# Exp behind the state chain's copies, mixer rows loaded later, the last batch's angles moved forward: one change to a fused recurrence and mixer kernel

## The chip, the cores and the metric

The kernel runs on one core of a Trainium2 chip. The core has a matrix engine (PE, with its weight loads shown as PEld), a vector engine (DVE), an activation engine (ACT), a general engine (POOL), an engine that issues transfers (SP), and 16 DMA engines. Each engine works through its own instructions in order and waits for others by semaphores. The metric is the device time of one execution in microseconds (us), as the median of several runs.

## The reference

A recurrence over 768 steps runs for 4 batches of 8 heads with a 40 x 40 state per head; its output feeds a mixer. Cut to what matters:

```python
for t in range(S):
    y[:, :, t] = einsum('bhd,bhde->bhe', rt, state)
    Sa = einsum('bhde,bhe->bhd', state, at)
    state_decay = state * wt[:, :, None, :] - einsum('bhd,bhe->bhde', Sa, bt)
    state = state_decay + einsum('bhd,bhe->bhde', vt, kt)
x = y as [batch, token, 320]
theta = x @ w_theta
zr, zi = x * cos(theta), x * sin(theta)
u = x + einsum('ts,bsd->btd', w_tok_r, zr) + einsum('ts,bsd->btd', w_tok_i, zi)
out = u + maximum(u @ w_ch, 0)
```

The two token matrices are 768 x 768, the two channel matrices 320 x 320.

## The kernel before

The 768 steps of a batch are cut into 6 chunks of 128, so there are 24 tiles, numbered 0 to 23 through the batches, and a loop of 24 iterations (lines 516 to 564). A tile's recurrence is written as matrix products inside the chunk plus a state `gt` handed from tile to tile. The loop is a software pipeline: iteration i loads the raw inputs of tile i+4, takes logarithm and decay sums of tiles i+3 and i+2, forms the scores of tile i+1, does the state step of tile i, and finishes the output of tile i-1 and the mixer angles of tile i-2.

**Preparation of a tile.** `load` issues six transfers of 160 KB from SP into the `raw` pool (three buffers). `prep_ln` takes the Ln of w on ACT (`lw`). `prep_csi` sums it on PE (L148) and takes the Exp on ACT (`invW`, L151); POOL multiplies k and b by it (`kb`, L155). `prep_cse` does the same for a second sum (`Wi`, `ah`). `prep_rv` casts r and v on POOL (`rv`, L143). `tr_kb`, `tr_a`, `tr_rv` transpose on PE (all show as L182) and copy out (`kbT`, `aT`, `rvT`); scores are formed on PE (L214) and masked on DVE (L222).

**The state chain of a tile.** `rec_x0` builds a product on PE, whose negative ACT copies as `nx` (L273). `rec_nu` takes it back to PE (L278, L281), and ACT copies `nu` (L285). `rec_gt` makes the next state. `nx` of tile i marks the beginning of iteration i in what follows.

**The mixer.** `moe_theta` multiplies a tile with w_theta, and ACT copies the angles (`th`, L424). Three tiles' cosines and sines are taken together (`moe_sines`, L443) in iterations 4, 7, 10, 13, 16, 19 and 22; they need another ACT table than Ln and Exp, so a table load stands before them, and `ln_exp_again` (L447) loads the Ln and Exp table right behind them. An iteration later POOL multiplies them with x (`moe_z`, L432: `zr`, `zi`). A row block of the mixer output sums twelve products of `wtok` and z (`y_part`, L453); it is added to x (`u`), transposed (L362), copied (`uT`), multiplied with w_ch (L410) and written out (`oo`, two buffers). Batch b's rows are made while later tiles run, one row block in an iteration from iteration 9 on; the last batch's six rows are made behind the loop.

The token matrices arrive as six row blocks each. A row block of both, here called a pair, is loaded by two transfers that POOL issues (`wtok_load`), and three buffers hold each matrix's blocks. Two iterations later PE transposes them (`wtok_trans`, L399) and DVE copies the result.

**What sets the order.** The program is written in the order of the loop, but a scheduler orders each engine's instructions by priorities and estimated times, and may move them past each other. Instructions wrapped in `keep_in_program_order` keep their order among themselves. PSUM has four small buffers (`sm`) and two large ones (`sc`), which are handed out in turn. ACT, POOL and PE never overtake inside one engine: an instruction that waits holds everything behind it.

## Time and profile before

| what | value |
|---|---|
| median of 3 runs | 260.32 us (259.92 to 261.09) |
| the profiled execution's own time | 262.26 us |
| its span, from first to last instruction | 260.5 us |
| mean granted PE clock | 0.949 |
| PE busy | 215.0 us, 83% |
| DVE busy | 185.4 us, 71% |
| ACT busy | 160.4 us, 62% |
| POOL busy | 120.9 us, 46% |
| DMA moved | 30.81 MB, nearly all in packets under 512 B |

A row of a timeline gives the start in us, the time that the instruction was busy, the engine (a small q behind it means the engine's sequencer, as for issued transfers), the line, the operation, the tiles out<-in with their shapes, and in square brackets how long the engine had been idle and what ended that. Matmuls are pipelined: their busy times overlap, so the distance between starts tells the pace. The digit lines of the page cut the span into 40 slices of 6.5 us.

### The profile page before, as it was taken

How to read it: one execution, taken by the hardware profiler on the slowest of the kernel's cores; microseconds unless marked ns; L12 is line 12 of the kernel's file. 1: busy time of each engine (PE TensorE's matmuls, PEld its weight loads, DVE VectorE, ACT ScalarE, POOL GpSimd, SP SyncE). 2: the span in 40 equal slices, each digit the busy share in tenths (PEclk: the TensorE clock that was granted, in tenths of full speed). 3: DMA queues.
4: the chain of work that ended last, by engine and by line, in shares of the span. 5: the costliest groups of instructions: out<-in, count | busy, mean ns of one | idle time of the engine just before them, and what ended most of it. 6: DMA issues, size and time to landing. Idle time of an engine off the chain costs nothing.

```text
span 260.5 us, 8110 instructions
## 1 busy us (share of the span) xinstructions
PE 215.0 (83%) x3368; PEld 167.8 (64%) x3368; DVE 185.4 (71%) x287; ACT 160.4 (62%) x303; POOL 120.9 (46%) x186
## 2 busy tenths in 40 slices
...
DMA  7999999999999898767697579645500001011012
GB/s 128 189 176 149 210 158 195 159 159 169 181 190 168 138 172 154 133 117 136 129 172 138 91 137 169 113 95 110 103 29 4 28 25 35 20 64 40 0 50 101
DMA packets 155685, 30.81 MB, mean 118 GB/s; under 512 B 150401, under 2 KB 155649, under 8 KB 155649
## 3 DMA queue, kind: packets, MB, share of 16 engines
...
q0 software_dynamic: 2432, 2.77, 6.4%
q8 instruction: 26, 0.43, 0.7%
q14 instruction: 11, 0.08, 0.1%
...
## 4 chain that ended last, share of the span: by engine, by line
PE 46%; ACT 15%; issue 12%; DMA 10%; POOL 9%; DVE 4%; SPq 3%; POOLq 0%; DVEq 0%; ACTq 0%
PE sm L453 10%; DMA raw_rv<-in_r_dram 9%; PE sm L182 7%; PE sc L214 6%; PE sm L410 5%; ACT cs L443 4%; SPq L128 3%; ACT L443 2%; ACT L447 2%; PE sc L453 2%; PE sm L362 2%; PE sm L349 2%; PE sm L278 2%; DVE lamu L222 1%; POOL kb_93 L155 1%
## 5 line engine op out<-in xcount | busy, mean ns | idle before, releaser
L103 ACT COPY rvT<-sm 128x1024 bf16<-128x1024 bf16 x18 | 18.2, 1013 | 26.0 <-PE sm L182 26.0
L453 PE MATMUL sm<-zr,wtok_r 128*128 128x320 bf16 x120 | 33.8, 304 | 0.0
L453 PE MATMUL sm<-zi,wtok_i 128*128 128x320 bf16 x120 | 33.7, 303 | 0.0
L222 DVE TENSOR_TENSOR psi<-sc,mask_p 128x1024 bf16<-128x1024 f32 x24 | 29.3, 1221 | 5.4 <-PE sc L214 5.1
L222 DVE TENSOR_TENSOR phi<-sc,mask_n 128x1024 bf16<-128x1024 f32 x24 | 29.1, 1214 | 0.0
L222 DVE TENSOR_TENSOR lamu<-sc,mask_p 128x1024 bf16<-128x1024 f32 x24 | 29.1, 1214 | 0.0
L222 DVE TENSOR_TENSOR lamv<-sc,mask_p 128x1024 bf16<-128x1024 f32 x24 | 29.1, 1214 | 0.0
L193 DVE COPY kbT<-sm 128x1024 bf16<-128x1024 bf16 x24 | 16.5, 687 | 14.7 <-PE sm L182 14.7
L331 ACT COPY nuT<-sm 128x512 bf16<-128x512 bf16 x24 | 14.0, 585 | 10.9 <-PE sm L182 10.8
L453 PEld LDWEIGHTS <-wtok_r 128*128 128x128 bf16 x144 | 14.4, 100 | 9.6 <-issue 3.9
L453 PEld LDWEIGHTS <-wtok_i 128*128 128x128 bf16 x144 | 14.3, 100 | 7.5 <-issue 1.9
L214 PE MATMUL sc<-aT,kbT 64*128 64x128 bf16 x384 | 18.8, 229 | 0.0
L273 ACT ACTIVATE nx<-sm 128x320 bf16<-128x320 f32 x24 | 10.4, 432 | 11.5 <-PE sm L269 11.5
L103 ACT COPY uT<-sm 128x384 bf16<-128x384 bf16 x18 | 8.5, 483 | 14.1 <-PE sm L362 14.1
L143 POOL CAST rv_96<-raw_rv 128x320 bf16<-128x320 f32 x12 | 5.4, 453 | 24.5 <-DMA raw_rv<-in_r_dram 21.8
L155 POOL TENSOR_TENSOR kb_93<-raw_kb,invW 128x320 bf16<-128x320 f32 x12 | 10.1, 866 | 13.2 <-ACT invW L151 13.2
L424 ACT COPY th<-sm 128x320 f32<-128x320 f32 x24 | 10.6, 441 | 8.6 <-PE sm L410 8.6
L200 ACT COPY aT<-sm 128x512 bf16<-128x512 bf16 x24 | 14.1, 587 | 2.0 <-PE sm L182 2.0
L155 POOL TENSOR_TENSOR kb_91<-raw_kb,invW 128x320 bf16<-128x320 f32 x10 | 8.4, 861 | 14.4 <-ACT invW L151 14.4
L410 PE MATMUL sm<-wch,uT 128*128 128x320 bf16 x72 | 14.3, 313 | 0.2 <-ACT uT L103 0.2
L174 ACT ACTIVATE Wi<-sm 128x328 f32<-128x328 f32 x24 | 10.7, 448 | 5.9 <-PE sm L168 3.1
L214 PEld LDWEIGHTS <-kbT 64*128 64x128 bf16 x384 | 11.9, 99 | 3.7 <-issue 2.9
...
## 6 DMA issues: line engine op xcount, KB each, us to landing
...
wtok_row_r<-in_moe_w_tok_r_dram POOLq DMA_DIRECT2D x6, 192.0 KB, 5.1
```

Of the source, the lines that this page charges most:

```text
L103: nc.scalar.copy(out=out, in_=in_)
L155: (nc.vector if i < 2 else nc.gpsimd).tensor_tensor(out=q.kbh[:, j, :, 0:D], in0=q.kb[:, j], in1=q.invW[:, 0], op=ALU.mult)
L174: nc.scalar.activation(out=q.Wi, in_=cse[:, 0:DM + 8], func=AF.Exp)
L182: nc.tensor.transpose(out=dst[:, g * 128:(g + 1) * 128], in_=src[:, 2 * g:2 * g + 2, :].rearrange("p a b -> p (a b)"), identity=ident)
L193: nc.vector.tensor_copy(out=q.kbT.rearrange("p a b -> p (a b)"), in_=pt)
L200: nc.scalar.copy(out=q.aT, in_=pt[:, 0:512])
L214: nc.tensor.matmul(P[:, p, g, :], lhsT=lhs[rows(p), g * 128:(g + 1) * 128], rhs=rhs[rows(p), g * 128:(g + 1) * 128], start=True, stop=True)
L222: nc.vector.tensor_tensor(out=s.rearrange("p a b c -> p (a b) c"), in0=P.rearrange("p a b c -> p (a b) c"), in1=mask.to_broadcast([128, 2 ...
L331: nc.scalar.copy(out=q.nuT, in_=pt[:, 0:512])
L410: nc.tensor.matmul(dst, lhsT=lhs[:, kt, :], rhs=rhs[:, kt, :], start=kt == 0, stop=kt == 2)
L443: tc.keep_in_program_order(nc.scalar.activation(out=cs[:, c, 0:n], in_=ths[bi][:, j0:j0 + n], func=AF.Sin, bias=(pi2_col[:, :], 0.0)[c]))
L453: nc.tensor.matmul(yp, lhsT=wtok[nm][:, sb, j * 128:(j + 1) * 128], rhs=z[:, sb], start=start and n == 0, stop=stop and n == 2 * len(sbs) - 1)
```

## The change

Four things are rewritten.

1. `prep_csi` (the Exp `invW`) is called behind `rec_nu` and `out_y`, no longer ahead of them. `prep_ln` of tile i+3 is called ahead of the sines, no longer at the iteration's end. The load of the Ln and Exp table is put off from right behind the sines to right ahead of the next `invW`, in the next iteration; where no `invW` follows, it falls away.
2. The mixer's pairs are loaded in iterations 3 to 8 and transposed in 6 to 11; before, they were loaded in 0 to 5 and transposed in 2 to 7. The number of buffers for them is unchanged.
3. The `raw` pool has four buffers; to pay for the room, `th` and `cs` have one buffer each and no longer two.
4. Behind the loop, the last tile's transposed x, angles, sines and z come ahead of most of the last batch's accumulation, the products of rows 4 and 5 are started with the others and not at the end, and the last tile's `zr` is made on DVE beside POOL's `zi`. All z products keep the program's order.

```diff
--- before.py
+++ after.py
@@ -83,7 +83,7 @@
     for i, t in sorted(to_zero, key=lambda e: e[0]):
         nc.vector.memset(t, 0.0)
 
-    raw = ctx.enter_context(tc.tile_pool(name="raw", bufs=3))
+    raw = ctx.enter_context(tc.tile_pool(name="raw", bufs=4))
     exps = ctx.enter_context(tc.tile_pool(name="exps", bufs=4))
     trs = ctx.enter_context(tc.tile_pool(name="trs", bufs=3))
     scs = ctx.enter_context(tc.tile_pool(name="scs", bufs=2))
@@ -91,6 +91,7 @@
     xp = ctx.enter_context(tc.tile_pool(name="xp", bufs=2))
     mw = ctx.enter_context(tc.tile_pool(name="mw", bufs=1))
     mk = ctx.enter_context(tc.tile_pool(name="mk", bufs=2))
+    mk1 = ctx.enter_context(tc.tile_pool(name="mk1", bufs=1))
     ps_sc = ctx.enter_context(tc.tile_pool(name="ps_sc", bufs=2, space=PSUM))
     ps_sm = ctx.enter_context(tc.tile_pool(name="ps_sm", bufs=4, space=PSUM))
 
@@ -142,14 +143,20 @@
             else:
                 nc.gpsimd.tensor_copy(out=q.rvb[:, j, :, 0:D], in_=q.rv[:, j])
 
+    reload = [False]
+
     def prep_csi(i):
         q = tiles[i]
         csi = tile_of(ps_sm, [128, 512], FP32, "sm")
         nc.tensor.matmul(csi[:, 0:DM], lhsT=ntri_inc, rhs=q.lw[:, :, 0:D],
                          start=True, stop=True)
+        if reload[0]:
+            ln_exp_again()
+            reload[0] = False
         q.invW = tile_of(exps, [128, 1, H, D], FP32, "invW")
-        nc.scalar.activation(out=q.invW.rearrange("p o h d -> p (o h d)"),
-                             in_=csi[:, 0:DM], func=AF.Exp)
+        tc.keep_in_program_order(nc.scalar.activation(
+            out=q.invW.rearrange("p o h d -> p (o h d)"), in_=csi[:, 0:DM],
+            func=AF.Exp))
         q.kbh = kb_t[i % NB]
         for j in range(2):
             (nc.vector if i < 2 else nc.gpsimd).tensor_tensor(
@@ -171,7 +178,8 @@
                              rhs=ones2, start=False, stop=True,
                              skip_group_check=True)
         q.Wi = tile_of(exps, [128, DM + 8], FP32, "Wi")
-        nc.scalar.activation(out=q.Wi, in_=cse[:, 0:DM + 8], func=AF.Exp)
+        tc.keep_in_program_order(nc.scalar.activation(
+            out=q.Wi, in_=cse[:, 0:DM + 8], func=AF.Exp))
         q.ah = ah_t[i % 2]
         (nc.vector if i < 2 else nc.gpsimd).tensor_tensor(
             out=q.ah[:, :, 0:D], in0=q.a,
@@ -418,26 +426,28 @@
 
         bi, j = divmod(i, NCH)
         if bi not in ths:
-            ths[bi] = tile_of(mk, [128, NT, DM], FP32, "th")
+            ths[bi] = tile_of(mk1, [128, NT, DM], FP32, "th")
         tp = tile_of(ps_sm, [128, 512], FP32, "sm")
         mix3(tp[:, 0:DM], tiles[i].xT, wth)
         nc.scalar.copy(out=ths[bi][:, j], in_=tp[:, 0:DM])
 
     cs_of = {}
 
-    def moe_z(bi, js):
+    def moe_z(bi, js, other=None):
         cs = cs_of[bi, js[0]]
         for m, j in enumerate(js):
             for c in range(2):
-                nc.gpsimd.tensor_tensor(out=zs[bi][c][:, j], in0=cs[:, c, m],
-                                        in1=tiles[bi * NCH + j].x, op=ALU.mult)
+                eng = other if other is not None and c == 0 else nc.gpsimd
+                tc.keep_in_program_order(eng.tensor_tensor(
+                    out=zs[bi][c][:, j], in0=cs[:, c, m],
+                    in1=tiles[bi * NCH + j].x, op=ALU.mult))
 
     def moe_sines(bi, js):
         if bi not in zs:
             zs[bi] = (tile_of(mk, [128, NT, DM], BF16, "zr"),
                       tile_of(mk, [128, NT, DM], BF16, "zi"))
         j0, n = js[0], len(js)
-        cs = tile_of(mk, [128, 2, 3, DM], FP32, "cs")
+        cs = tile_of(mk1, [128, 2, 3, DM], FP32, "cs")
         cs_of[bi, j0] = cs
         for c in range(2):
             tc.keep_in_program_order(nc.scalar.activation(
@@ -522,10 +532,10 @@
         nxt(tr_a, i + 1)
         if i > 1:
             moe_theta(i - 2)
-        nxt(prep_csi, i + 2)
         rec_nu(i)
         if i > 0:
             out_y(i - 1)
+        nxt(prep_csi, i + 2)
         nxt(prep_cse, i + 2)
         nxt(sc_psiphi, i + 1)
         out_nut(i)
@@ -533,11 +543,12 @@
         nxt(ev_phi, i + 1)
         if i > 0:
             out_xt(i - 1)
+        nxt(prep_ln, i + 3)
         due = None
         if sines:
             due = (bi, (0, 1, 2)) if ci == 4 else (bi - 1, (3, 4, 5))
             moe_sines(*due)
-            ln_exp_again()
+            reload[0] = True
             busy_act[0] = True
         for m in prev:
             moe_ch(*m)
@@ -553,11 +564,10 @@
         busy_act[0] = False
         if i == 0:
             moe_weights()
-        if i < NCH:
-            wtok_load(i)
-        if 2 <= i < NCH + 2:
-            wtok_trans(i - 2)
-        nxt(prep_ln, i + 3)
+        if 3 <= i < NCH + 3:
+            wtok_load(i - 3)
+        if 6 <= i < NCH + 6:
+            wtok_trans(i - 6)
         if z_due:
             moe_z(*z_due)
         z_due = due
@@ -571,26 +581,26 @@
     acc = [tile_of(ps_sc, [128, 2, 512], FP32, "sc") for _ in range(2)]
     yps = [acc[j // 2][:, j % 2, 0:DM] for j in range(4)]
     for j in range(2):
-        y_part(yps[j], B - 1, j, range(NT - 1), True, False)
+        y_part(yps[j], B - 1, j, range(3), True, False)
     out_xt(N - 1)
+    for j in range(2):
+        y_part(yps[j], B - 1, j, range(3, NT - 1), False, False)
+    moe_theta(N - 1)
+    moe_sines(B - 1, (5,))
+    moe_z(B - 1, (5,), nc.vector)
     for j in range(2, 4):
         y_part(yps[j], B - 1, j, range(NT - 1), True, False)
-    moe_theta(N - 1)
-    moe_sines(B - 1, (5,))
-    moe_z(B - 1, (5,))
-    for j in range(NT):
-        if j < 4:
+    for j in range(4, NT):
+        yps.append(tile_of(ps_sm, [128, 512], FP32, "sm")[:, 0:DM])
+        y_part(yps[j], B - 1, j, range(NT - 1), True, False)
+    for j in range(NT + 2):
+        if j < NT:
             y_part(yps[j], B - 1, j, (NT - 1,), False, True)
             y_evac(yps[j], B - 1, j)
-        else:
-            moe_y(B - 1, j)
-        if j > 0:
+        if 0 < j <= NT:
             moe_ut(B - 1, j - 1)
         if j > 1:
             moe_ch(B - 1, j - 2)
-    moe_ut(B - 1, NT - 1)
-    moe_ch(B - 1, NT - 2)
-    moe_ch(B - 1, NT - 1)
 
 
 # ---- launch: one core; inputs and outputs as the reference has them ----
```

**POOL, where tile 8 comes in (iterations 5 and 6).** `rv_97` and `kb_93` belong to tile 7, `rv_94` and `kb_90` to tile 8, `rv_95` to tile 9; x_102 to x_104 are tiles 0 to 2. Before:

```order
L143 CAST rv_97<-raw_rv 128x8x40 x2
L375 DMA wtok_row_r<-in_moe_w_tok_r_dram 128x768
L375 DMA wtok_row_i<-in_moe_w_tok_i_dram 128x768
L432 TENSOR_TENSOR zr<-cs,x_102 128x320
L432 TENSOR_TENSOR zi<-cs,x_102 128x320
L432 TENSOR_TENSOR zr<-cs,x_103 128x320
L432 TENSOR_TENSOR zi<-cs,x_103 128x320
L432 TENSOR_TENSOR zr<-cs,x_104 128x320
L432 TENSOR_TENSOR zi<-cs,x_104 128x320
L143 CAST rv_94<-raw_rv 128x8x40 x2
L155 TENSOR_TENSOR kb_93<-raw_kb,invW 128x8x40 x2
L176 TENSOR_TENSOR ah_89<-raw_a,Wi 128x8x40
```

Ahead of these rows stand five pairs, so the one shown is the last. In the change this piece is the same but for the second cast of tile 8, which goes behind tile 7's `ah`, and only two pairs stand ahead of it. The other three follow here (`rv_96` and `kb_92` are tile 10, `kb_91` is tile 9, `rv_97` tile 11, the last `rv_94` tile 12):

```order
L144 CAST rv_95<-raw_rv 128x8x40 x2
L383 DMA wtok_row_r<-in_moe_w_tok_r_dram 128x768
L383 DMA wtok_row_i<-in_moe_w_tok_i_dram 128x768
L144 CAST rv_96<-raw_rv 128x8x40 x2
L162 TENSOR_TENSOR kb_91<-raw_kb,invW 128x8x40 x2
L184 TENSOR_TENSOR ah_89<-raw_a,Wi 128x8x40
L383 DMA wtok_row_r<-in_moe_w_tok_r_dram 128x768
L383 DMA wtok_row_i<-in_moe_w_tok_i_dram 128x768
L144 CAST rv_97<-raw_rv 128x8x40 x2
L162 TENSOR_TENSOR kb_92<-raw_kb,invW 128x8x40 x2
L184 TENSOR_TENSOR ah_88<-raw_a,Wi 128x8x40
L144 CAST rv_94<-raw_rv 128x8x40 x2
```

Two pairs, the fourth and the fifth, stand among the tiles 9 to 11; the sixth follows the last row shown, and six z products follow it.

**ACT, around the sines of iteration 13.** Before:

```order
L331 COPY nuT<-sm 128x512
L103 COPY xT_3059<-sm 128x384
L443 ACT_TABLE_LOAD
L443 ACTIVATE cs<-th,pi_col 128x960
L443 ACTIVATE cs<-th 128x960
L447 ACT_TABLE_LOAD
L134 ACTIVATE lw_86<-raw_w 128x8x40
L273 ACTIVATE nx<-sm 128x320
L200 COPY aT<-sm 128x512
L424 COPY th<-sm 128x320
L151 ACTIVATE invW<-sm 128x320
L285 CAST nu_98<-sm 128x8x40
```

In the change:

```order
L339 COPY nuT<-sm 128x512
L104 COPY xT_3062<-sm 128x384
L135 ACTIVATE lw_86<-raw_w 128x8x40
L453 ACT_TABLE_LOAD
L453 ACTIVATE cs<-th,pi_col 128x960
L453 ACTIVATE cs<-th 128x960
L281 ACTIVATE nx<-sm 128x320
L208 COPY aT<-sm 128x512
L432 COPY th<-sm 128x320
L293 CAST nu_98<-sm 128x8x40
L457 ACT_TABLE_LOAD
L157 ACTIVATE invW<-sm 128x320
```

The Ln has gone ahead of the sines; the table load that stood between sines and Ln has gone behind `nx`, `aT`, `th` and `nu`, and `invW` behind it.

**PE, at the last tile's angles.** xT_5258 and xT_5252 are the last tile's x, transposed, wth the angles' weights. Before:

```order
L410 LDWEIGHTS xT_5258
L410 MATMUL sm<-wth,xT_5258 128x320
L453 LDWEIGHTS wtok_r
L453 MATMUL sc<-zr,wtok_r 128x320
L453 LDWEIGHTS wtok_r
L453 MATMUL sc<-zr,wtok_r 128x320
L453 LDWEIGHTS wtok_i
L453 MATMUL sc<-zi,wtok_i 128x320
L453 LDWEIGHTS wtok_i
L453 MATMUL sc<-zi,wtok_i 128x320
```

These four products are the first of the eight of rows 0 to 3 with the last tile's z; all 40 products of these rows with the other five tiles stand ahead, and rows 4 and 5 follow whole at the very end. In the change:

```order
L418 LDWEIGHTS xT_5252
L418 MATMUL sm<-wth,xT_5252 128x320
L463 LDWEIGHTS wtok_r
L463 MATMUL sc<-zr,wtok_r 128x320
L463 LDWEIGHTS wtok_i
L463 MATMUL sc<-zi,wtok_i 128x320
L463 LDWEIGHTS wtok_r
L463 MATMUL sc<-zr,wtok_r 128x320
```

Here 20 of the products stand ahead of the angles, and these are the first of 40 that follow before any needs the last tile's z.

## The prediction

> **What bounds the kernel now.** I read the page first, then busy time by stage, then the waits and the timelines of the stages that stand out.
>
> ```profile
> span 260.5 us, 8110 instructions
> DMA  7999999999999898767697579645500001011012
> q0 software_dynamic: 2432, 2.77, 6.4%
> wtok_row_r<-in_moe_w_tok_r_dram POOLq DMA_DIRECT2D x6, 192.0 KB, 5.1
> 18.00:76.00 58.00, 43.27 (x736) 34.44 (x735) 39.66 (x49) 33.81 (x67) 35.58 (x56) 0.89 1.03 174
> 126.00:134.50 8.50, 8.31 (x143) 6.55 (x141) 7.30 (x10) 5.40 (x14) 3.35 (x5) 1.00 0.74 145
> 134.50:143.00 8.50, 7.97 (x137) 6.26 (x135) 7.75 (x12) 8.02 (x13) 5.29 (x8) 1.00 0.74 137
> 246.00:260.50 14.50, 10.19 (x64) 6.31 (x62) 5.03 (x11) 2.87 (x6) 0.00 (x0) 0.74 0.19 68
> ```
>
> The window rows give time, then PE, PEld, DVE, ACT and POOL busy, the granted clock, DMA share and GB/s. There are three stages. Until about 84 us the DMA engines are full (nines; 1.03 in the second stage row). In the middle PE is nearly full, 8.31 of 8.50 us in a plain iteration, and ACT joins it where sines run (8.02). The end has a granted clock of 0.74 and little else busy. So the change is worth a different thing in each stage: bytes, then ACT order, then waits.
>
> The loading stage, POOL first, then what waits for it:
>
> ```profile
> 0.75 0.42 SPq L128 DMA_DIRECT2D raw_w<-in_w_dram  x1
> 22.93 0.56 SPq L128 DMA_DIRECT2D raw_w<-in_w_dram  x1
> 61.28 0.45 POOL L143 CAST rv_97<-raw_rv 128x320 bf16<-128x320 f32 x1 [2.92 <-DMA raw_rv<-in_r_dram]
> 62.50 0.60 POOL L375 DMA_DIRECT2D wtok_row_r<-in_moe_w_tok_r_dram  x1
> 67.38 0.78 POOL L432 TENSOR_TENSOR zi<-cs,x_104 128x320 bf16<-128x320 f32 x1
> 69.47 0.45 POOL L143 CAST rv_94<-raw_rv 128x320 bf16<-128x320 f32 x1 [1.31 <-DMA raw_rv<-in_r_dram]
> 70.52 1.67 POOL L155 TENSOR_TENSOR kb_93<-raw_kb,invW 128x320 bf16<-128x320 f32 x2
> 74.68 0.45 POOL L143 CAST rv_95<-raw_rv 128x320 bf16<-128x320 f32 x1 [1.67 <-DMA raw_rv<-in_r_dram]
> 75.75 0.44 ACT L273 ACTIVATE nx<-sm 128x320 bf16<-128x320 f32 x1 [8.98 <-PE sm L269]
> L273 ACT ACTIVATE nx<-sm x24: 418/437/470, 18.7 to 223.4; 128x320 bf16<-128x320 f32 x24
> ```
>
> POOL runs in order. The cast of tile 8's r (69.47) stands ahead of tile 7's k and b product (70.52), so iteration 6's nx, at 75.75, hangs on the landing of tile 8, 6.3 us before it. Four tiles' loads are issued in 22.93 - 0.75 = 22.2 us, 5.5 us a tile. Tile 8's r landed 8.2 us after tile 7's, with one mixer pair issued between; tile 9's 5.2 us after tile 8's, with none. The last of the six mixer pairs is issued at 62.50. The last row gives the whole loop: nx of iteration 0 at 18.7, of iteration 23 at 223.4.
>
> **The loads (mixer rows three iterations later, raw tiles four deep).** Queue q0 took 6.4% of 260.5 = 16.7 us of all engines for 2.77 MB; the twelve row blocks of 192 KB are 2.36 MB of it, so a pair costs 16.7 x 2.36/2.77 / 6 = 2.37 us. In the new POOL order only pairs 0 to 2 stand ahead of tile 8's r, where six did. Tile 8 lands 3 x 2.37 = 7.1 us earlier. The z products in between do not take over: they end at 68.2 now, ahead of the cast, and start behind tile 7's casts, which come 7.1 us earlier too. **Term: -7.1 us** at iteration 6. If the pairs do not delay a tile that is already queued, one pair more comes off (-9.5); if only two of the three get out of the way, one less (-4.7). The fourth raw buffer frees a slot one iteration earlier, but SP issues without a pause in this stage, so I give it nothing.
>
> The Trainium skill's "DMA: Bandwidth & Descriptors" (section on queues, rings and completion order) has each DMA engine take turns between the queues that have work, packet by packet. The 8.2 us between two tiles with one pair between them agrees: the pair is paid at once, not behind the backlog, which is why -9.5 is only an end.
>
> What is moved must be paid. A pair's transposes, in the chain of waits, and the nx behind them:
>
> ```profile
> 82.47 0.72 PE sm L399 x11
> ...
> 83.62 0.45 ACT nx L273
> ```
>
> Iterations 2 to 5 lose them in a stage that waits for DMA anyway; iterations 8 to 11, PE full, gain them: 4 x 0.72 = **+2.9 us** (0 if hidden, no more than that). The late pairs need a row buffer that is freed by the transposes of three pairs earlier. On POOL, pair 5 waits for those of iteration 8, about 0.8 us ahead of the next nx as here. Its issue and the six z products behind it take 68.16 - 62.50 = 5.7 us, a cast 0.45, then comes tile 11's k and b product, 1.67: it ends about 7.0 us after nx. PE wants such a product 5.65 us after nx (row 140.39 below, nx at 134.74). **+1.4 us**, between 0 and 4.
>
> **The Exp, the Ln and the table load.** A sine iteration, ACT and PE, and the plain one before it:
>
> ```profile
> 132.35 1.01 ACT L103 COPY rvT<-sm 128x1024 bf16<-128x1024 bf16 x1 [1.97 <-PE sm L182]
> 134.74 0.44 ACT L273 ACTIVATE nx<-sm 128x320 bf16<-128x320 f32 x1
> 135.84 0.49 ACT L151 ACTIVATE invW<-sm 128x320 f32<-128x320 f32 x1
> 136.17 0.48 ACT L285 CAST nu_99<-sm 128x320 bf16<-128x320 f32 x1
> 136.40 1.69 POOL L155 TENSOR_TENSOR kb_93<-raw_kb,invW 128x320 bf16<-128x320 f32 x2 [3.79 <-ACT invW L151]
> 140.39 0.61 PE L182 MATMUL sm<-ident,kb_93 128*128 128x128 bf16 x8
> 141.90 1.28 ACT L447 ACT_TABLE_LOAD   x1
> 143.19 0.47 ACT L134 ACTIVATE lw_86<-raw_w 128x320 bf16<-128x320 f32 x1
> 143.57 0.42 ACT L273 ACTIVATE nx<-sm 128x320 bf16<-128x320 f32 x1
> 144.04 0.57 PE L410 MATMUL sm<-wth,xT_3059 128*128 128x320 bf16 x3 [1.43 <-ACT nx L273]
> ```
>
> Now the load of the Ln/Exp table (1.28) and the Ln (0.38 from start to start) lie between the sines and nx, and PE idles 1.43 us. In the change the Ln goes ahead of the sines, so these start 0.38 later, and the table load goes behind nx, aT, th and nu: nx comes 1.28 us earlier. That holds for the sine iterations 7, 10, 13, 16 and 19 (4 lies in the loading stage; at 22 nx waits for PE). I take 1.2 of the 1.43 each: 5 x 1.2 = **-6.0 us**, between 0, if the delayed Exp hands the wait on, and 5 x 1.43 = -7.2.
>
> In plain iterations the Ln leaves its place ahead of nx for one where ACT idles (1.97 before rvT). PE has 8.50 - 8.31 = 0.2 us to gain; about ten such iterations, **-2.0 us** (0 to -3.7, ten times the Ln). The Exp behind nu comes about 0.8 us later. What hides it: kb_93 is done at 138.09 and PE reads it at 140.39, 2.3 us of slack. In the iteration after sines the reload adds 1.28, and 0.2 us are left; the z products on POOL end at about that time, now as before. Cost nothing, with a rival below.
>
> **The end.**
>
> ```profile
> 232.87 1.28 ACT L443 ACT_TABLE_LOAD   x1
> 237.41 0.30 PE L453 MATMUL sc<-zi,wtok_i 128*128 128x320 bf16 x1 [0.93 <-POOL zi L432]
> 238.15 0.30 PE L453 MATMUL sc<-zi,wtok_i 128*128 128x320 bf16 x1 [0.31 <-POOL zi L432]
> 244.01 0.43 PE L453 MATMUL sc<-zr,wtok_r 128*128 128x320 bf16 x2 [2.04 <-POOL zr L432]
> 246.58 0.47 PE L453 MATMUL sc<-zr,wtok_r 128*128 128x320 bf16 x1
> 246.84 0.47 PE L453 MATMUL sc<-zi,wtok_i 128*128 128x320 bf16 x1
> 251.33 0.30 PE L453 MATMUL sm<-zr,wtok_r 128*128 128x320 bf16 x1
> 251.47 0.30 PE L453 MATMUL sm<-zi,wtok_i 128*128 128x320 bf16 x1
> 255.37 1.77 DMA out_dram<-oo
> 257.27 0.49 DVE L477 SCALAR_TENSOR_TENSOR oo<-sm,u_116 128x320 f32<-128x320 f32 x1 [1.12 <-DMA out_dram<-oo]
> ```
>
> PE waits 0.93 + 0.31 us for the z of tiles 3 and 4, then 2.04 for tile 5's. Behind that its steps are 0.26 us apart (246.58 to 246.84), later 0.14; a mean clock of 0.74 over the last 14.5 us, with these two speeds alone, is 7.5 us at half, and costs 3.8 us, of which I count 3.0 since part of it was waits. In the change iteration 22 loads no Ln/Exp table, since no Exp follows, so the Sin load at 232.87 falls: its 1.28 covers the 1.24 of waits. Tile 5's angles go ahead of most of the accumulation: 40 products of rows 2 to 5 at 0.14 = 5.6 us then cover the 2.04, and with no idle stretch there is no slow one. Sum -1.24 - 2.04 - 3.0 = -6.3. The other way round: from the last z of tile 4, now 1.28 earlier at 236.9, theta and 52 products take 7.7 us, to 244.6; the first row's oo comes at about 245.2 (an estimate, rows 0 to 3 finishing early). Two oo buffers, each held 0.49 + 1.77 us, allow a row every 1.13 us, so the sixth oo starts at 250.9 and ends at 251.4, and the 2.7 us from the last oo to the end as now (260.5 - 257.76) give 254.1: -6.4. **Term: -6.4 us**, between -3.4 (the slow clock stays) and -8 (outputs not held back).
>
> The Trainium skill's "ScalarE: Activation LUTs" (section on what a table load costs) counts a drain of about 1.38 us on top of 1.28. Here the Ln starts 0.01 us after its load ends, so the row decides; by the page the dropped Sin load would be worth 2.66, an estimate, and the sum about 241.8.
>
> **Sum** against the profiled execution: 260.5 - 7.1 + 2.9 + 1.4 - 6.0 - 2.0 - 6.4 = 243.3 us of span. The median of the runs, 260.32, stands 0.2 under the profiled span (that run's own time was 262.26), so **243.1 us**.
>
> **Rivals.**
> (a) The middle gives nothing: PE is the bound there, 8.3 of 8.5 us, and whatever ACT frees comes back as waits for kb. For it: 0.2 us of slack after a reload. Against: the 1.43 us idle names ACT's nx. Then 243.1 + 8.0 = 251.1. Chance 0.14.
> (b) The end keeps its slow clock, because PE's sparse last rows idle it again: 243.1 + 3.0 = 246.1. Against: forty dense products ahead. Chance 0.12.
> (c) All six pairs leave the way of tile 8, since with four raw buffers the tiles are queued ahead of them: another 3 x 2.37 off, 236.0. For it: the fourth buffer. Against: the pair that delayed tile 8 (8.2 us against 5.2) was issued behind queued tiles too. Chance 0.08.
> (d) Slower than before: the state chain gets nu sooner, but Exp, k and b product, transpose, kbT and scores become the longer circle. Its place is PE's transpose of kb, its price the Exp's delay beyond 2.3 us of slack in each of 22 iterations. To eat the 17 us the delay has to exceed 2.3 + 17/22 = 3.1 us, against 0.8 worked out. Then over 262. Chance 0.04.
> (e) The loads do not matter: the same bytes must land by iteration 9, and the loading stage ends when it ended; with the transposes added and the middle's gain lost to that, only the end's 6.4 us remain: 253.9. Against: what holds iteration 6 is one landing 6.3 us before its nx, and the nines last only to 84 us. Chance 0.06.
> The forecast has 0.56. **Range** 237 to 251: nearly from (c) to (a); (d) and (e) and the ends of (a) and (c) are left out. With about 0.5% (1.3 us) as what a measurement here can tell from no change: faster 0.94, the same 0.02, slower 0.04.
>
> **What will show it.** Right: iteration 6's nx near 68.6 instead of 75.75; no PE wait of 1.4 us behind nx in sine iterations, and these no longer than the plain ones; nx of iteration 23 near 212 (now 223.4, less 11.7); no wait over 1 us on tile 5's z and a clock over 0.9 up to the last products. Wrong: POOL waits on Exp over 3 us followed by PE waits on kb; POOL's row loads waiting over 5 us with kb behind them; or a half-clock stretch in the last 20 us.

## The result and the profile after

| | before | changed | ratio |
|---|---|---|---|
| median | 260.12 us (4 runs, 259.16 to 261.09) | 249.74 us (4 runs, 248.68 to 252.36) | 0.9616, 95% interval 0.9533 to 0.9698 |
| profiled execution, span | 260.5 us | 246.9 us | |
| granted PE clock | 0.949 | 0.967 | |

The change makes the kernel 10.4 us faster. 243.1 was forecast: the sign and the range are right, and 6.6 us of the gain did not come. Two things have to be kept apart. The two spans differ by 13.6 us, the medians by 10.4: the profiled execution of before (262.26) stood 2.1 above the median of its runs, that of the changed kernel (248.68) 1.1 below. So stage by stage, between the two traces, 13.6 is what there is to find, and 3.2 of it is not the change. In all that follows, runs over 1.5% above the fastest of the same kernel count as slow and are left out of ratios and intervals, and out of the medians of the variants.

The page of the changed kernel (slices of 6.2 us), and the group of its `nx` copies (shortest, median and longest in ns, then the first and last start):

```profile
span 246.9 us, 8107 instructions
PEclk9999999995699799999999999999999999999997
DMA  7998999999999999999998769645000000111012
...
L281 ACT ACTIVATE nx<-sm x24: 415/437/470, 18.6 to 214.9; 128x320 bf16<-128x320 f32 x24
```

The DMA engines now stay full to about 130 us (21 slices), where they eased at 84: bytes that were moved are still bytes. The half-clock stretch at the end is gone, one around 60 us is left (the 5 and the 6 among the digits). The last `nx` starts at 214.9, before at 223.4.

The `nx` copies in the ACT timeline (start, duration, what ACT waited for):

```profile
54.29 0.41 ACT L281 ACTIVATE nx<-sm 128x320 bf16<-128x320 f32 x1
66.02 0.44 ACT L281 ACTIVATE nx<-sm 128x320 bf16<-128x320 f32 x1 [5.76 <-PE sm L277]
...
112.46 0.44 ACT L281 ACTIVATE nx<-sm 128x320 bf16<-128x320 f32 x1 [2.71 <-PE sm L277]
```

These are iterations 5, 6 and 11. Four stages follow from such rows of both traces (before: 75.75, 118.0 and 223.4 for iterations 6, 11 and 23):

| stage | before | changed | difference | forecast |
|---|---|---|---|---|
| to `nx` of iteration 6 | 75.7 | 66.0 | -9.7 | -7.1 |
| iterations 6 to 10 | 42.3 | 46.4 | +4.2 | +1.3 (2.9 + 1.4, less two sine iterations at 1.2 and three plain ones at 0.2) |
| iterations 11 to 22 | 105.4 | 102.4 | -3.0 | -5.0 (three sine iterations, seven plain) |
| from `nx` of iteration 23 to the end | 37.1 | 32.0 | -5.1 | -6.4 |
| sum | 260.5 | 246.9 | -13.6 | -17.2 |

The first stage overshot, the other three fell short. The second is the surprise: it *lost* 4.2 us, and iteration 5 (54.29 to 66.02) still took 11.7 (14.8 before) where its neighbours take 7.4 and 8.2. POOL's timeline of this place and of iteration 9, then PE's row that waits there before the change and those of the changed kernel:

```profile
60.41 0.78 POOL L441 TENSOR_TENSOR zi<-cs,x_104 128x320 bf16<-128x320 f32 x1
61.66 0.45 POOL L144 CAST rv_94<-raw_rv 128x320 bf16<-128x320 f32 x1 [0.47 <-DMA raw_rv<-in_r_dram]
62.07 1.67 POOL L162 TENSOR_TENSOR kb_93<-raw_kb,invW 128x320 bf16<-128x320 f32 x2
...
90.84 0.45 POOL L144 CAST rv_94<-raw_rv 128x320 bf16<-128x320 f32 x1 [1.69 <-DMA raw_rv<-in_v_dram]
91.35 0.59 POOL L383 DMA_DIRECT2D wtok_row_r<-in_moe_w_tok_r_dram  x1
...
96.25 0.78 POOL L441 TENSOR_TENSOR zi<-cs,x_107 128x320 bf16<-128x320 f32 x1
96.98 0.44 POOL L144 CAST rv_95<-raw_rv 128x320 bf16<-128x320 f32 x1
97.39 1.66 POOL L162 TENSOR_TENSOR kb_93<-raw_kb,invW 128x320 bf16<-128x320 f32 x2
```

```profile
71.43 0.61 PE L182 MATMUL sm<-ident,kb_93 128*128 128x128 bf16 x4 [6.33 <-POOL kb_93 L155]
...
62.98 0.61 PE L190 MATMUL sm<-ident,kb_93 128*128 128x128 bf16 x4 [3.82 <-POOL kb_93 L162]
...
98.29 0.40 PE L190 MATMUL sm<-ident,kb_93 128*128 128x128 bf16 x4 [0.47 <-POOL kb_93 L162]
99.11 0.40 PE L190 MATMUL sm<-ident,kb_93 128*128 128x128 bf16 x4 [0.42 <-POOL kb_93 L162]
```

Both times the k and b product of the tile that PE wants next stands behind six z products and behind a cast of a *later* tile that waits for a landing. In the first place the landing did come 7.8 us earlier than before (cast at 61.66, before 69.47), as forecast; but the z products end at 61.2, half a us before it, so that both hold the product, and PE still waits 3.82 us (6.33 before). Whether this order on POOL is the cause is what the later experiments ask.

### The profile page after: what moved, and what is told of

It reads as the page before. It is cut to its first block, busy times and chain, and to the rows that moved or that the text cites. A ratio compares the mean times of both kernels' runs of the same rounds, so it can differ in the third digit from the quotient of the medians.

```text
span 246.9 us, 8107 instructions
## 1 busy us (share of the span) xinstructions
PE 211.6 (86%) x3368; PEld 165.9 (67%) x3368; DVE 186.6 (76%) x288; ACT 156.9 (64%) x301; POOL 120.7 (49%) x185
## 4 chain that ended last, share of the span: by engine, by line
PE 51%; issue 13%; POOL 12%; DMA 11%; DVE 5%; ACT 5%; SPq 2%; POOLq 0%; DVEq 0%; ACTq 0%
PE sm L463 12%; PE sm L190 9%; PE sc L222 7%; DMA raw_rv<-in_v_dram 7%; PE sm L418 5%; DMA raw_rv<-in_r_dram 3%; PE sm L370 2%; ACT nx L281 2%; SPq L129 2%; PE sc L463 2%; PE sm L357 2%; POOL kb_93 L162 2%; PE sm L286 2%; POOL zi L441 2%; DMA out_dram<-oo 1%
## 5 line engine op out<-in xcount | busy, mean ns | idle before, releaser
L463 PE MATMUL sm<-zi,wtok_i 128*128 128x320 bf16 x120 | 33.1, 299 | 0.5 <-POOL zi L441 0.5
L463 PE MATMUL sm<-zr,wtok_r 128*128 128x320 bf16 x120 | 33.1, 299 | 0.4 <-POOL zr L441 0.4
L222 PE MATMUL sc<-aT,kbT 64*128 64x128 bf16 x384 | 20.9, 233 | 0.0
L339 ACT COPY nuT<-sm 128x512 bf16<-128x512 bf16 x24 | 14.1, 586 | 10.5 <-PE sm L190 10.4
L162 POOL TENSOR_TENSOR kb_92<-raw_kb,invW 128x320 bf16<-128x320 f32 x12 | 10.1, 867 | 12.8 <-ACT invW L157 12.7
L222 PEld LDWEIGHTS <-kbT 64*128 64x128 bf16 x384 | 13.1, 101 | 3.4 <-issue 2.5
L162 POOL TENSOR_TENSOR kb_93<-raw_kb,invW 128x320 bf16<-128x320 f32 x12 | 10.1, 860 | 9.5 <-ACT invW L157 9.5
L354 PEld LDWEIGHTS <-lamv 128*128 128x128 bf16 x192 | 14.1, 96 | 0.2
L289 PEld LDWEIGHTS <-phi 128*128 128x128 bf16 x192 | 8.4, 96 | 8.6 <-issue 6.5
L418 PE MATMUL sm<-wch,uT 128*128 128x320 bf16 x72 | 13.4, 299 | 0.9 <-ACT invW L157 0.3
```

Of the source, the lines that this page charges most:

```text
L162: (nc.vector if i < 2 else nc.gpsimd).tensor_tensor(out=q.kbh[:, j, :, 0:D], in0=q.kb[:, j], in1=q.invW[:, 0], op=ALU.mult)
L222: nc.tensor.matmul(P[:, p, g, :], lhsT=lhs[rows(p), g * 128:(g + 1) * 128], rhs=rhs[rows(p), g * 128:(g + 1) * 128], start=True, stop=True)
L339: nc.scalar.copy(out=q.nuT, in_=pt[:, 0:512])
L354: nc.tensor.matmul(o, lhsT=q.lamv[:, p, g, :], rhs=q.kbh[:, 0, h, 0:D], start=first, stop=False, skip_group_check=True)
L418: nc.tensor.matmul(dst, lhsT=lhs[:, kt, :], rhs=rhs[:, kt, :], start=kt == 0, stop=kt == 2)
L463: nc.tensor.matmul(yp, lhsT=wtok[nm][:, sb, j * 128:(j + 1) * 128], rhs=z[:, sb], start=start and n == 0, stop=stop and n == 2 * len(sbs) - 1)
```

## The experiments

Each was timed against the kernel before, on the same chip. Medians, with the ratio to before (259.7 to 260.2 in these series) and its 95% interval:

| run | median | ratio | interval |
|---|---|---|---|
| changed kernel | 249.74 | 0.9616 | 0.9533 to 0.9698 |
| before + mixer rows moved | 257.99 | 0.9935 | 0.9902 to 0.9969 |
| before + raw tiles four deep | 259.94 | 1.0000 | 0.9955 to 1.0045 |
| before + ACT order | 255.19 | 0.9830 | 0.9754 to 0.9905 |
| before + end | 257.26 | 0.9900 | 0.9813 to 0.9986 |
| changed, rows early as before | 250.28 | 0.9635 | 0.9594 to 0.9677 |
| changed, transposes one iteration sooner | 254.03 | 0.9772 | 0.9718 to 0.9826 |
| changed, z products ahead of the row pair | 251.41 (two runs) | 0.9678 | 0.9585 to 0.9772 |
| changed, no transposes of the rows | 257.38 | 0.9902 | 0.9868 to 0.9936 |
| changed, fixed POOL order | 242.64 | 0.9318 | 0.9267 to 0.9368 |
| the same, rows early as before | 244.06 | 0.9377 | 0.9320 to 0.9434 |
| before + fixed POOL order | 252.28 | 0.9669 | 0.9575 to 0.9763 |
| fixed POOL order, transposes off the sine iterations | 239.64 | 0.9193 | 0.9146 to 0.9239 |

And where the time lies, from the `nx` rows of each trace (us between `nx` of the iterations named; "end" is from `nx` of iteration 23 to the end of the span; the marks are read to 0.1 us, so a difference can be off by 0.1):

| trace | to 7 | 7 to 11 | 11 to 23 | end | span |
|---|---|---|---|---|---|
| before | 83.6 | 34.4 | 105.4 | 37.1 | 260.5 |
| changed | 73.4 | 39.1 | 102.4 | 32.0 | 246.9 |
| before + rows moved | 73.7 | 40.3 | 105.3 | 36.2 | 255.6 |
| before + raw tiles four deep | 82.8 | 34.5 | 106.9 | 36.3 | 260.4 |
| before + ACT order | 82.4 | 32.7 | 102.1 | 37.6 | 254.8 |
| before + end | 81.8 | 34.5 | 105.4 | 32.7 | 254.3 |
| changed, rows early | 82.1 | 32.6 | 102.2 | 32.0 | 248.8 |
| changed, fixed POOL order | 70.0 | 36.7 | 102.4 | 32.0 | 241.1 |
| the same, rows early | 76.0 | 32.4 | 102.2 | 32.0 | 242.6 |
| before + fixed POOL order | 75.8 | 34.5 | 105.4 | 36.0 | 251.7 |
| fixed order, transposes off the sines | 69.2 | 33.3 | 103.4 | 32.0 | 237.9 |

### One part at a time

The mixer rows alone:

```diff
-        if i < NCH:
-            wtok_load(i)
-        if 2 <= i < NCH + 2:
-            wtok_trans(i - 2)
+        if 3 <= i < NCH + 3:
+            wtok_load(i - 3)
+        if 6 <= i < NCH + 6:
+            wtok_trans(i - 6)
```

> The kernel before with only the mixer rows and their transposes moved (rows in iterations 3 to 8, transposes in 6 to 11); three raw buffers, ACT order and end as before. Forecast theory (the moved pairs alone clear the way of tile 8): nx of iteration 6 at 68.6 instead of 75.75, iterations 8 to 11 longer by 2.9 + 1.4, so 260.3 - 7.1 + 4.3 = 257.5 us. Rival A (the moved work costs what the changed kernel showed, 6.1 us more in iterations 8 to 11, from 33.2 to 39.3, by itself): about 257 to 260, with nx of iteration 6 below 69 and iterations 8 to 11 at 38 or more. Rival B (the loading stage's gain of 9.7 needs the fourth raw buffer): nx of iteration 6 not below 71, and the time not below 259.

257.99 us, 1.7 faster. `nx` of iteration 6 came at 65.4, with three raw buffers: rival B falls. Iterations 8 to 11 (from `nx` of 8 to `nx` of 12, the marks of that forecast: 33.2 before) took 38.5, between the 37.5 of the forecast and the 39.3 of the changed kernel; with its 38 or more and its 257 to 260 us, rival A holds, narrowly. POOL of this kernel in iteration 5 and PE's row that waits there, then POOL from the end of iteration 7 to iteration 9:

```profile
60.73 0.78 POOL L432 TENSOR_TENSOR zi<-cs,x 128x320 bf16<-128x320 f32 x1
61.47 1.67 POOL L155 TENSOR_TENSOR kb<-raw_kb,invW 128x320 bf16<-128x320 f32 x2
63.09 0.44 POOL L143 CAST rv<-raw_rv 128x320 bf16<-128x320 f32 x1
```

```profile
62.38 0.61 PE L182 MATMUL sm<-ident,kb 128*128 128x128 bf16 x4 [5.02 <-POOL kb L155]
```

```profile
82.24 0.45 POOL L143 CAST rv<-raw_rv 128x320 bf16<-128x320 f32 x1 [3.86 <-DMA raw_rv<-in_r_dram]
...
87.62 0.78 POOL L432 TENSOR_TENSOR zi<-cs,x 128x320 bf16<-128x320 f32 x1
88.36 0.44 POOL L143 CAST rv<-raw_rv 128x320 bf16<-128x320 f32 x1
88.77 1.67 POOL L155 TENSOR_TENSOR kb<-raw_kb,invW 128x320 bf16<-128x320 f32 x2
...
98.33 0.46 POOL L143 CAST rv<-raw_rv 128x320 bf16<-128x320 f32 x1 [4.80 <-DMA raw_rv<-in_v_dram]
98.75 1.68 POOL L155 TENSOR_TENSOR kb<-raw_kb,invW 128x320 bf16<-128x320 f32 x2
```

The stall ahead of `nx` of iteration 6 has not gone: PE still waits 5.02 us, here behind the z products alone, since the cast of tile 8 follows the product. Two smaller ones of the same build (z products, a waiting cast, and behind them k and b) have come 27 and 37 us later, where PE waits 2.21 and 0.61 us.

The raw tiles alone:

```diff
-    raw = ctx.enter_context(tc.tile_pool(name="raw", bufs=3))
+    raw = ctx.enter_context(tc.tile_pool(name="raw", bufs=4))
...
-            ths[bi] = tile_of(mk, [128, NT, DM], FP32, "th")
+            ths[bi] = tile_of(mk1, [128, NT, DM], FP32, "th")
```

(`cs` likewise; `mk1` is a pool of one buffer.)

> The kernel before with only the raw tiles four deep (theta and the cosines and sines in one buffer to pay for it). Forecast theory: nothing, 260.3, nx of iteration 6 within 0.8 us of 75.75, since SP issues without a pause in the loading stage. Rival B (the fourth buffer brings what the loading stage gained beyond 7.1, or more): nx of iteration 6 at 73.3 or earlier, 257.9 or less. Rival C (single buffers of theta and of the cosines and sines make the sines or theta wait): 261 to 263, with waits on cs or th in the sine iterations.

259.94 us, no difference; `nx` of iteration 6 at 74.9, 0.9 earlier. It was worth nothing, and cost nothing. (Iteration 14 of its trace took 1.5 us longer than before, at a granted clock of 0.84; no other trace has that.)

The ACT order alone:

```diff
-        nxt(prep_csi, i + 2)
         rec_nu(i)
         if i > 0:
             out_y(i - 1)
+        nxt(prep_csi, i + 2)
...
+        nxt(prep_ln, i + 3)
         due = None
...
-            ln_exp_again()
+            reload[0] = True
```

(The put-off table load in `prep_csi` and the fixed order of the Exps as in the change; the old call of `prep_ln` falls away.)

> The kernel before with only the new order on ACT (Exp behind the state chain's copies, Ln ahead of the sines, the table load behind nx, aT, th and nu). Forecast theory: 260.3 - 6.0 - 2.0 = 252.3, sine iterations 1.2 us shorter and plain ones 0.2. Rival A (the middle gives about what the changed kernel showed in iterations 12 to 23, 2.9 us, plus as much again in proportion for 4 to 11): 255 to 257, sine iterations 0.7 shorter, plain ones not at all. Rival D (the later Exp makes the k and b product the longer circle): 260 or more, and PE waits on kb of more than 0.5 us in plain iterations.

255.19 us, 4.5 faster (2.5 to 6.4 by the interval): rival A, not the forecast. The period that holds the sines of iteration 13 ends, in the ACT timeline of this kernel, with:

```profile
123.08 0.44 ACT L280 ACTIVATE nx<-sm 128x320 bf16<-128x320 f32 x1
131.42 0.46 ACT L280 ACTIVATE nx<-sm 128x320 bf16<-128x320 f32 x1
139.42 0.44 ACT L280 ACTIVATE nx<-sm 128x320 bf16<-128x320 f32 x1 [0.17 <-PE sm L276]
```

8.0 us with sines, where before took 8.83 (134.74 to 143.57); the plain period ahead of it 8.34, before 8.47. Over the loop from iteration 7 on, the five sine periods gain 1.5, 0.8, 0.8, 0.8 and 0.8 = 4.7 us, all others together 0.2. In the last four PE waits 0.30 us behind `nx`, as in plain iterations. In iteration 7 it still waits 1.16 us behind `nx` and 0.67 behind `aT`; before, the wait there was another one (1.99 us, on DVE's copy `gd`). Rival D falls: from iteration 8 on no single wait of PE on k and b reaches 0.5 us.

The end alone: z of the last tile shared with DVE, and

```diff
     for j in range(2):
-        y_part(yps[j], B - 1, j, range(NT - 1), True, False)
+        y_part(yps[j], B - 1, j, range(3), True, False)
     out_xt(N - 1)
-    for j in range(2, 4):
-        y_part(yps[j], B - 1, j, range(NT - 1), True, False)
+    for j in range(2):
+        y_part(yps[j], B - 1, j, range(3, NT - 1), False, False)
     moe_theta(N - 1)
     moe_sines(B - 1, (5,))
-    moe_z(B - 1, (5,))
+    moe_z(B - 1, (5,), nc.vector)
...
```

with the other rows behind, as in the change.

> The kernel before with only the new end (order of the last accumulation, z of tile 5 shared with DVE; the order of the z products kept). The Ln/Exp table is still loaded behind iteration 22's sines, so the Sin load of 1.28 us stays. Forecast theory: from nx of iteration 23 to the end 37.1 - 6.4 + 1.2 = 31.9, so about 255.1. Rival A (the clock stays slow, 3.0 us not won): 34.9, 258.1. Rival E (the last rows are held by the outputs, so that every wait removed in front is given back there): 36 or more, 259.5 to 260.3.

257.26 us, 2.4 faster (0.4 to 4.9 by the interval). In its trace `nx` of iteration 23 starts at 221.6 and the span ends at 254.3: 32.7 from there to the end, where 31.9 was forecast and 37.1 was before. In the changed kernel, without the Sin load, it is 32.0: the load was worth 0.7 of its 1.28, by one trace of each.

The four parts make 1.7 + 0 + 4.5 + 2.4 = 8.6 us; with the 0.7 for the Sin load 9.3 of the 10.4. What is left is within the intervals.

### Which of the moved loads' costs

The rows early again, all else as changed (the first diff, reversed):

> The changed kernel with the row pairs loaded and transposed as early as before (four raw buffers, ACT order and end as changed). It prices the moved loads inside the whole change. If the parts add up (4.5 us for the ACT order and 2.4 for the end, as they measured alone): 260.1 - 6.9 = 253.2, so the moved loads with the fourth buffer are worth 3.5. If the moved loads are worth no more than alone (1.7): 251.4. If they are a loss inside the whole: under 249.5. nx of iteration 6 at 74 to 76 in each case, and the three periods to iteration 11 at about 25.

250.28 us: within the spread of 249.74. Inside the whole change the moved rows are worth nothing that can be told. POOL and PE of this kernel, iteration 5:

```profile
66.23 0.78 POOL L441 TENSOR_TENSOR zi<-cs,x 128x320 bf16<-128x320 f32 x1
68.19 0.45 POOL L144 CAST rv<-raw_rv 128x320 bf16<-128x320 f32 x1 [1.18 <-DMA raw_rv<-in_r_dram]
68.89 0.45 POOL L144 CAST rv<-raw_rv 128x320 bf16<-128x320 f32 x1 [0.24 <-DMA raw_rv<-in_v_dram]
69.30 1.67 POOL L162 TENSOR_TENSOR kb<-raw_kb,invW 128x320 bf16<-128x320 f32 x2
```

```profile
70.21 0.61 PE L190 MATMUL sm<-ident,kb 128*128 128x128 bf16 x4 [6.42 <-POOL kb L162]
```

One stall of 6.42 us, as before; behind it the loop runs without any on k and b (32.6 for iterations 7 to 10). With the rows late the stall is smaller (3.82 us), but in iteration 9 PE waits 0.9 us for z and 0.9 for k and b, and in iteration 10 1.71 us for DVE's copy `gd`.

The transposes left out:

```diff
-    wrow = ctx.enter_context(tc.tile_pool(name="wrow", bufs=3))
+    wrow = ctx.enter_context(tc.tile_pool(name="wrow", bufs=6))
...
+    for nm in ("r", "i"):
+        nc.vector.memset(wtok[nm], 0.0)
...
-        if 6 <= i < NCH + 6:
-            wtok_trans(i - 6)
```

> The changed kernel with the transposes of the token matrices left out, and so their evacuations on DVE (the matrices are zero instead, so the mixer's part of the output is not the reference's); the loads stay where they are, with six row buffers. It prices the transposes. In the changed kernel's profile the periods that end with nx of iterations 9, 10 and 11 take 9.0 + 11.3 + 10.8 = 31.1 us, against 24.7 with the new ACT order alone. Theory 1 (the transposes with their evacuations are all of it): these three periods fall to about 25 and the time to 249.7 - 6.4 = 243.3. Theory 2 (only the 0.72 us of PE of a pair, four times): 28.2 and 246.8. Theory 3 (the loads themselves, by DMA and POOL's order, are the cost): 30 or more, and 248.5 to 250.

257.38 us, slower than with the transposes: the edit also gives the row blocks six buffers and zeroes the matrices, and the experiment did not measure what it was made for. The zeroing holds DVE for 2 x 1.98 us at the start, `nx` of iteration 1 comes at 37.3 instead of 25.9, and another POOL order results, in which PE waits 7.70 us for one k and b product behind six z products. The three periods to iteration 11 do take 23.9 us, as theory 1 said, but the loop is 16 us behind by then (`nx` of iteration 7 at 89.6) and its loads have landed, so that this proves little.

The transposes one iteration sooner, and the z products ahead of the pair's transfers:

```diff
-        if 6 <= i < NCH + 6:
-            wtok_trans(i - 6)
+        if 5 <= i < NCH + 5:
+            wtok_trans(i - 5)
```

> The changed kernel with each pair's transposes one iteration sooner (iterations 5 to 10). The row buffers come free an iteration sooner, so POOL no longer waits for them, and one pair's transposes more lies where PE waits for loads. Theory 1 (transposes cost where PE is full, about 1.6 us a pair): 249.7 - 1.6 = 248.1, with POOL's row loads waiting under 0.3 us. Theory 2 (only the wait of the last pair for its row buffer matters): 248.3, the same number, but with the period of iteration 10 to 11 unchanged at 10.8 and the one before it down by 1.4. Theory 3 (the work is only moved): 249.2 to 250.2.

```diff
+        if z_due:
+            moe_z(*z_due)
         if 3 <= i < NCH + 3:
             wtok_load(i - 3)
         if 6 <= i < NCH + 6:
             wtok_trans(i - 6)
-        if z_due:
-            moe_z(*z_due)
```

> The changed kernel with the z products issued ahead of the row pair's load on POOL, where both fall in one iteration (the third pair and the sixth). The forecast's chain (sixth pair late, z products late, k and b product late, PE waits 4 x 0.45 us for it): the period that ends with nx of iteration 10 falls from 11.3 by 1.4 to 1.8 and the time to about 248.1. Rival (the k and b product was late because tile 12's landing held POOL's cast in front of it, and DVE behind it is full): under 0.5 us off, 249.2 to 250.

254.03 and 251.41 us. The first is *slower* than the changed kernel, by 4.3 us, which no theory had. The second cannot be told from it: its two runs took 250.07 and 252.75 us (the changed kernel's 248.68 to 252.36), and the intervals overlap; what is sure is that the 248.1 of its forecast did not come. The traced executions took 257.19 and 253.99 us; what is read from them is an order, which is the same in each. POOL of the first in iteration 8, of the second in iteration 9:

```profile
95.14 0.45 POOL L144 CAST rv<-raw_rv 128x320 bf16<-128x320 f32 x1 [2.45 <-DMA raw_rv<-in_r_dram]
95.56 1.67 POOL L162 TENSOR_TENSOR kb<-raw_kb,invW 128x320 bf16<-128x320 f32 x2
```

```profile
100.50 0.45 POOL L144 CAST rv<-raw_rv 128x320 bf16<-128x320 f32 x1 [5.83 <-DMA raw_rv<-in_r_dram]
100.91 1.68 POOL L162 TENSOR_TENSOR kb<-raw_kb,invW 128x320 bf16<-128x320 f32 x2
```

In these executions PE waits 4.75 and 3.68 us for these products. In the second the z products are out of the way, and a cast whose tile is two further on waits 5.83 us for its landing, with the product of the present tile ready behind it. The scheduler had put it there: a small edit elsewhere changes its order, and the stall changes its place and size. So each of the two holders has been seen alone: z products in iteration 5 of the kernel with only the rows moved, a cast here. That made the order itself the suspect.

### The order on POOL

The casts, the k and b product and the a product of one tile are held in the program's order, casts first, and the z products are cut in two:

```diff
+                tc.keep_in_program_order(
+                    nc.gpsimd.tensor_copy(out=q.rvb[:, j, :, 0:D], in_=q.rv[:, j]))
...
+        if z_due:
+            moe_z(*z_due, part=slice(0, 2))
+        nxt(prep_rv, i + 2)
         nxt(prep_csi, i + 2)
         nxt(prep_cse, i + 2)
...
-        nxt(prep_rv, i + 2)
         for m in yrows:
...
+        if z_due:
+            moe_z(*z_due, part=slice(2, 3))
```

(The two products are wrapped as the casts are; the call of the z products at the iteration's end falls away, so the row pair comes last.)

> The changed kernel with another order on POOL: in each iteration the r and v casts, the k and b product and the a product of the same tile, fixed in this order, and of the six z products four ahead of them and two behind them, the row pair last. So no cast of a later tile, and at most three us of z products, stand ahead of a k and b product. Theory P (what iterations 9 to 11 lose is the k and b product standing on POOL behind z products and a later tile's cast): the 31.1 us of the three periods to nx of iteration 11 fall to 26.5 (three times 8 plus three pairs' transposes), nx of iteration 6 stays at 66 or earlier, and the time falls by 4 to 6, to 244 to 246. Rival Q (the transposes and the landings themselves cost it): three periods of 30 or more, 248.5 to 250.5. Rival R (the fixed order costs more than it wins, because a cast or a z product now waits in front of work that was ready): over 251, with POOL waits on landings followed by PE waits on kb.

> The same fixed POOL order in the variant that loads and transposes the row pairs as early as before (250.3 with the planner's order; there nx of iteration 6 comes 16.0 us after the one before it, PE waiting 6.4 us for kb_). Theory P: that period falls to about 9.6, and the time to 250.3 - 6.4 = 243.9; then moved loads are worth nothing beyond the order on POOL (both variants within 1.5 us). Rival Q (tile 8's landing is what is late, whatever POOL does): the period stays at 14 or more, and the time at 249 to 251, and the moved loads are worth the difference to the other run.

242.64 and 244.06 us. Theory P holds, by more than it said. POOL and PE of the first at the place of the old stall:

```profile
56.32 0.45 POOL L145 CAST rv<-raw_rv 128x320 bf16<-128x320 f32 x1
58.00 0.45 POOL L145 CAST rv<-raw_rv 128x320 bf16<-128x320 f32 x1 [1.23 <-DMA raw_rv<-in_v_dram]
58.41 1.67 POOL L163 TENSOR_TENSOR kb<-raw_kb,invW 128x320 bf16<-128x320 f32 x2
```

```profile
59.33 0.40 PE L195 MATMUL sm<-ident,kb 128*128 128x128 bf16 x4 [0.42 <-POOL kb L163]
```

The product starts at 58.41, 3.7 us earlier than in the changed kernel, and PE waits 0.42 for it instead of 3.82. In the second variant the period to iteration 6 falls from 16.0 to 9.2 us, though tile 8's v lands at 68.0 instead of 68.8. So at this place it was the order, not the landing, that PE had to wait for. With the order fixed, loading the rows late is worth 1.4 us (the intervals overlap). Not all of P came true: the periods to iterations 9, 10 and 11 took 28.7 us instead of 26.5, the last of them still 10.8; 3.4 of the 5.8 us between the traces lay ahead of iteration 7. The edit does three things at once (casts held at their tile, z products cut in two, the row pair last); what each is worth was not measured.

Is it the change's doing? The same order in the kernel before, nothing else (its z products are held in order too, as in the change):

> The kernel before with the fixed POOL order alone; nothing of the change is in it. Before, nx of iteration 6 comes 14.7 us after nx of iteration 5, with tile 8's r cast and six z products ahead of tile 7's k and b product. Theory P (the stall is POOL's order and was in the kernel before already, so neither the mixer rows nor the ACT order caused it): that period falls to about 9, and the time to 260.0 - 5.5 = 254.5 (253.5 to 255.5), more than the moved rows won alone (1.7). Rival Q (the fixed order only helps together with the changed ACT order, since Exp comes earlier in the old one): 258.5 to 260.5, the period still 13 or more, or 0.5 us more in other iterations.

252.28 us, 7.9 faster, more than expected; the period to iteration 6 is 7.7 us instead of 14.8. The stall was in the kernel before. One edit of POOL's order is worth three quarters of the whole change.

The 10.8 us that are left, from `nx` of iteration 10 to `nx` of 11, in the stage rows (window, its length, PE, PEld, DVE, ACT and POOL busy, granted clock, DMA share, GB/s) of the fixed order with the rows late, and then with the rows early:

```profile
95.90:106.70 10.80, 8.73 (x156) 7.25 (x154) 10.22 (x16) 7.24 (x13) 6.07 (x10) 1.00 1.02 176
```

```profile
100.30:108.40 8.10, 8.01 (x141) 6.39 (x140) 7.24 (x11) 7.05 (x13) 3.37 (x5) 1.00 1.01 172
```

PE waits there for a copy that DVE makes late, which it does not with the rows early:

```profile
106.15 0.20 PE L276 MATMUL sm<-gt,aT 128*128 128x80 bf16 x1 [1.71 <-DVE gd L102]
```

DVE is busy 10.22 of 10.80 us: in a sine iteration it makes the copies that ACT makes otherwise, a mixer row adds its own, and three copies of 0.55 us from two pairs' transposes fall into this window. So the transposes go where there are no sines:

```diff
-        if 3 <= i < NCH + 3:
-            wtok_load(i - 3)
-        if 6 <= i < NCH + 6:
-            wtok_trans(i - 6)
+        if i in (3, 4, 5, 6, 7, 9):
+            wtok_load((3, 4, 5, 6, 7, 9).index(i))
+        if i in (5, 6, 8, 9, 11, 12):
+            wtok_trans((5, 6, 8, 9, 11, 12).index(i))
```

> The changed kernel with the fixed POOL order (242.6), and the pairs' transposes kept out of the iterations with sines (in 5, 6, 8, 9, 11, 12 instead of 6 to 11; row loads in 3, 4, 5, 6, 7, 9). With the fixed order the period from nx of iteration 10 to nx of 11 is still 10.8 us, where sines, a mixer row and a pair's transposes fall together; without the transposes there it was 8.2. Theory S (the three together make that period long, the small accumulators waiting for DVE): 10.8 falls to 8.2 to 8.6, two periods grow by 0.7, so 242.6 - 1.3 = 241.3, or 240.9 as POOL no longer waits for row buffers. Rival (the transposes cost the same wherever PE is full, or tile 12's and 13's landings decide): 242 to 243.5.

239.64 us, 8.1% faster than before and 4.0% faster than the changed kernel: the best of all. The same period:

```profile
94.20:102.50 8.30, 7.94 (x144) 6.57 (x142) 7.72 (x12) 7.25 (x13) 3.40 (x5) 1.00 1.06 175
```

8.3 us with DVE at 7.72, and no wait on `gd`: theory S. (The edit also loads the last pair one iteration later; POOL's wait for a row buffer had cost nothing, as said below.) The time fell by 3.0 us where 1.3 to 1.7 was expected; the granted clock over the whole span is 0.995, in the run it is compared with 0.972.

## Why the prediction was right and where it was wrong

**Right in sign, for mostly the reasons given; that the time lies inside the range, 1.3 us from its upper end, owes something to luck.** The first stage gave 2.6 us more than its term, the other three 6.2 less. The landing that iteration 6 hung on came about as much earlier as forecast (cast at 61.66 instead of 69.47, 7.8 against 7.1); the fourth raw buffer was worth nothing; the late Exp hurt nobody (rival d); the clock of the end is full up to the last products (rival b); the changed kernel is not at 236 (rival c). `nx` of iteration 23 came at 214.9, 8.5 earlier; the terms ahead of it add to 10.8, so the 11.7 given as a sign was a slip.

**The loads: -7.1 + 2.9 + 1.4 = -2.8 forecast, -1.7 measured alone, -0.5 (not to be told from 0) inside the whole.** The first term came, and for its reason. Besides tile 8's landing, tile 4's r came 4.3 us earlier with two pairs fewer ahead of it (cast at 32.47 instead of 36.81; 2 x 2.37 = 4.7), and `nx` of iteration 7 is 9.9 us earlier with the rows moved alone, 8.7 inside the whole. The sentence that the z products "do not take over" held in the changed kernel by half a us only: they end at 61.2, the cast starts at 61.66. With the rows moved alone they did take over. What the prediction did not see is that the landing was one of two holders: the stall was read as one late landing, and was POOL's order, with a cast and six z products ahead of a product that needs neither. The fixed order takes both away, and is worth 7.1 us on the changed kernel, 6.2 with the rows early, 7.9 on the kernel before. The step that failed is the price of the moved transposes. Iterations 7 to 10 took 39.1 us with the rows late and 32.6 with them early, 6.5 for what was priced at 4.3. With POOL's order fixed it is 36.7 - 32.4 = 4.3: by difference, the 2.2 between are the order again, at new places. And the 4.3 are not made as forecast, 0.72 us of PE a pair and a wait for a row buffer. POOL's late pairs wait for buffers (2.16 and 1.28 us in the fixed order), but behind them POOL still waits 1.23 and 1.16 us for the Exp, so nothing is lost. What costs is DVE's copy in the sine iteration: with the transposes out of there, 33.3 - 32.4 and 103.4 - 102.2 leave 2.1 us for all six. DVE's two copies a pair were not counted at all.

**The first stage's extra 2.6 us** stand in rows that the sum put at nothing. Of it, 0.7 is the landing itself (7.8 against 7.1). Another 0.6 is tile 8's second cast, which no longer stands ahead of tile 7's product: from the start of the first cast to the product it is 1.05 us before and 0.41 in the change. And 1.3 is the transposes of a pair, which before stood between PE's work on that product and `nx`:

```profile
74.09 0.72 PE L399 MATMUL sm<-ident,wtok_row_r 128*128 128x128 bf16 x5
74.60 0.85 PE L399 MATMUL sm<-ident,wtok_row_i 128*128 128x128 bf16 x6
```

From PE's first row on `kb_93` to `nx` it is 4.32 us before (71.43 to 75.75) and 3.04 in the change (62.98 to 66.02). It is 3.04 with the rows alone moved too, and 4.32 in the changed kernel with the rows early. "Iterations 2 to 5 lose them in a stage that waits for DMA anyway" was wrong here: these stand behind the landing. All this is one pair of traces, and executions differ at both ends of the span: with the same code there, `nx` of iteration 7 comes at 83.6 before and at 81.8 in the kernel with the new end alone, and the last stage is 37.1 before and 36.2 and 36.0 in the kernels with the rows moved and with the fixed order. The prediction's sum was made from one execution that stood 2.1 us above the median.

**ACT's order: -8.0 forecast, -4.5 measured.** The sine iterations were right in mechanism: in four of the five, PE's wait behind `nx` fell from 1.43 to 0.30 us in the changed kernel (iteration 7 had no such wait before),

```profile
133.67 1.28 ACT L453 ACT_TABLE_LOAD   x1
...
137.12 0.44 ACT L281 ACTIVATE nx<-sm 128x320 bf16<-128x320 f32 x1 [0.17 <-PE sm L277]
```

with only the sines' own table load left ahead of `nx`. But 0.30 is left, as in a plain iteration, and PE is then full (second number, of the period's 8.00 us):

```profile
129.10:137.10 8.00, 7.91 (x138) 6.25 (x136) 7.27 (x11) 7.11 (x13) 4.23 (x7) 1.00 0.96 173
```

So five gave 4.7 and not 6.0. The plain iterations were mis-sized: 0.2 us each was put on the Ln, out of an idle PE share of 8.50 - 8.31; they gave 0.2 in all. ACT had waited for PE there, so taking work from ACT could not help. Rival (a) was the nearest of the five: the middle gave not nothing but half.

**The end: -6.4 forecast, -5.1 between the traces (some 4 against the 36.2 and 36.0 above); alone, with the Sin load kept, -2.4 by the medians.** The wait on the last z and the slow clock went. The waits on tile 4's z did not go with the Sin load:

```profile
227.64 0.30 PE L463 MATMUL sc<-zr,wtok_r 128*128 128x320 bf16 x1 [0.41 <-POOL zr L441]
228.39 0.30 PE L463 MATMUL sc<-zi,wtok_i 128*128 128x320 bf16 x1 [0.45 <-POOL zi L441]
```

0.86 us of the 1.24 is still there, since the sines come behind copies of `uT` and `th` that wait for PE, not behind the load alone. The rows then leave at the pace that was worked out: the first `oo` starts at 237.73 and the last ends at 244.18, 6.45 us against 6.2.

**The sum.** Of the 6.6 us that are missing, 3.6 are these terms (13.6 against 17.2 between traces), and 3.2 come from setting one execution against medians, less the 0.2 that the prediction allowed for it.

Rival (e), that the same bytes must land by iteration 9, gave 253.9 with a chance of 0.06. Its half on the loads is close to what happened, its half on the middle is not, and its reason does not hold: with the rows early and POOL's order fixed, the same bytes ahead of it let iteration 6 start at 68.6 instead of 74.5, and at 68.4 instead of 75.7 in the kernel before.
